# Projecting attention features in native float32 on TensorE's two halves, in place of a block-diagonal split product

## The chip, the cores and the metric

The kernel runs as one program on one core of a Trainium2 chip. Its time is the device time of one execution in microseconds (us), as the median of three executions. The core's engines are TensorE (PE for its matmuls and PEld for its weight loads in the profile), VectorE (DVE), ScalarE (ACT), GpSimd (POOL) and the SyncE queue (SP), which issues all DMAs of the kernel before the change.

## The reference

The inputs are q, k, v of shape (4 batches, 8 heads, 576 positions, 64), omega (128 features x 64), and the weights of two feed-forward layers (512 to 2048 to 512). What is computed is linear attention with random features, followed by the two layers on all 2304 tokens:

```python
def phi(x):                      # x is q or k, scaled by 64 ** -0.25
    proj = einsum('bhsd,md->bhsm', x, omega)
    h = proj - sum(x * x) / 2
    return exp(h - max(h)) / sqrt(m)
kv  = einsum('bhsm,bhsd->bhmd', phi(k), v);  z = sum(phi(k), axis=2)
num = einsum('bhsm,bhmd->bhsd', phi(q), kv)
den = einsum('bhsm,bhm->bhs', phi(q), z) + 1e-06
x = num / den                    # then transposed to (2304, 512)
h = x @ w_in;   x = (h * clip(h + 3, 0, 6) / 6) @ w_out      # layer 1
h = x @ w2_in;  x = (h * sigmoid(1.702 * h)) @ w2_out        # layer 2
```

## The kernel before

**Tiles.** The 576 positions of a batch are cut into 512 main ones (four blocks of 128) and 64 leftover ones. Main positions of each batch are one column block of 512 for the layers; the leftovers of all four batches together are a fifth block of 256 columns, which is worked on along with the last batch. The hidden width 2048 is cut into 16 chunks of 128.

**Precision.** Matmuls of the layers run in the fp32r type on split operands: a number is kept as a high part (rounded to fp32r) and a low part (the rest), and a product is three matmuls, high x high, high x low and low x high. The feature projection is done in the same way. The positions of a q or k block arrive as [128 rows, 128 positions], where rows 0 to 63 hold the 64 dimensions of one block of positions and rows 64 to 127 those of another. `bd_hi` and `bd_lo` hold omega as a block-diagonal pair [128, 2, 128], so that one matmul over all 128 rows gives 256 columns: the features of both position blocks, one after the other. Half of that operand is zeros. `T` (lines 266 and 267) makes the high and low parts of a head's q and k on VectorE, `PJ(h, 0)` projects k and `PJ(h, 1)` projects q with six 256-column matmuls each (`project`, line 225), and `features` takes the maximum on VectorE (L231) and four exponentials on ScalarE (L233). `TL` and `PL` are the same for the leftovers. Transposes (`QT` L315, `QTL` L260, `XT` L367, `XTL` L374), the products with v (`KV`, L292 and L300) and the numerators (`NU`, L329 and L338) are native float32 matmuls already. Outputs of 64 partitions are put into the lower and the upper half in turn in `KV` and `NU`; those of L338 all go to the lower half.

**Stages.** The attention of batch 0 runs first, with little else to fill in. Then come the units of the layers: layer 1 for batches 0, 1 and 2, then batch 3 and the leftovers, then layer 2 in the same order, 16 chunks for each. `emit_h` does the first product of a chunk (L439, twelve matmuls of 512 columns), `emit_o` the second product two chunks later (L501). While layer 1 works on batch n, the attention steps of batch n+1 are put between: `side()` is called twice in `emit_h` and twice in `emit_o`, and each call takes one step off the list until it is empty (57 steps). A call lies after six or twelve matmuls of 512 columns, so most steps stand alone between layer matmuls. Weights of both layers are converted during layer 1 (`convert_w`), with work on ScalarE, VectorE and GpSimd; what is not held on chip goes to DRAM and is fetched again.

**Order.** Each engine runs its instructions in one fixed order. The framework settles it when the program is built, from the order of the program and a planned timeline; `tc.issue_after` (`behind` in the code) adds a wish that one instruction is put behind another. PSUM has eight banks of [128, 512]: four in the pool `acc`, four in `psp`. During layer 1 the `acc` banks hold the second product's sums, and `emit_h` and all attention steps share the four banks of `psp`.

**The end.** `put` copies a result out of PSUM into `ob` and stores it. The leftover results (two tiles, each of two batches with 64 positions) are stored by one DMA each into a [2, 64, 512] piece of the output (L534); all other stores write 128 whole rows (L529).

Of the kernel before, what the change touches and what calls it, by code (L numbers as in the profile page):

```python
# [45 lines left out]
def performer_moe_kernel(  # L47
# [13 lines left out]
    nc = tc.nc  # L61
# [17 lines left out]
    TAIL = 12  # L79
    WARM = 8  # L80
    FIRST = 4
    HELD = 10
# [16 lines left out]
    bd_hi = const.tile([P, 2, M], F32R, name="bd_hi")  # L99
    bd_lo = const.tile([P, 2, M], F32R, name="bd_lo")  # L100
# [137 lines left out]
    class Att:  # L238
        def __init__(self, b, x, xl):
            self.b, self.x, self.xl = b, x, xl  # L240
            self.t, self.e, self.kv, self.xt, self.feat = {}, {}, {}, {}, {}

        def TL(self):
            a, self.vl = lqkv.pop(self.b)
            self.lhi = at.tile([P, NPAIR, P], F32R, tag="thi", bufs=2, name="lhi")
            self.llo = at.tile([P, NPAIR, P], F32R, tag="tlo", bufs=2, name="llo")
            self.split_in(self.lhi, self.llo, a)
            self.el = at.tile([P, NPAIR, 2, M], F32, tag="el", name="el")

        def PL(self, g):  # L250
            ps = bank([P, 4, M], "ps")
            for i in range(2):
                j = 2 * g + i
                project(ps[:, 2 * i:2 * i + 2, :], self.lhi[:, j, :], self.llo[:, j, :])
            features(ps, self.el[:, 2 * g:2 * g + 2].rearrange("p i j m -> p (i j) m"))

        def QTL(self):
            ps = bank([P, NPAIR, P], "ps")
            for i in range(NPAIR):
                nc.tensor.transpose(ps[:, i, :], self.el[:, i, 0, :], ident)  # L260
# [4 lines left out]
        def split_in(self, hi, lo, a):  # L265
            nc.vector.tensor_copy(hi, a)
            nc.vector.tensor_tensor(out=lo, in0=a, in1=hi.bitcast(F32), op=ALU.subtract)

        def T(self, h):
            a = qkv[self.b, h // 2][0][:, h % 2]  # L270
            hi = at.tile([P, 2, 2, P], F32R, tag="thi", bufs=2, name="thi")
            lo = at.tile([P, 2, 2, P], F32R, tag="tlo", bufs=2, name="tlo")
            self.split_in(hi, lo, a)
            self.t[h] = (hi, lo)

        def PJ(self, h, j):
            hi, lo = self.t[h]
            ps = bank([P, R, M], "ps")
            for g in range(2):
                project(ps[:, 2 * g:2 * g + 2, :], hi[:, j, g, :], lo[:, j, g, :])  # L280
            e = at.tile([P, R, M], F32, tag=f"e{j}", bufs=2, name="e")
            self.feat[h] = features(ps, e)
            self.e[h, j] = e

        def KV(self, h):
            i, p0 = h // 2, 64 * (h % 2)
            vv = qkv[self.b, i][1]
            e = self.e.pop((h, 0))
            ps = bank([P, D + 1], "ps")
            for r in range(R):  # L290
                for m0 in (0, 64):
                    nc.tensor.matmul(  # L292
                        out=ps[m0:m0 + 64, :],
                        lhsT=e[:, r, m0:m0 + 64],
                        rhs=vv[:, h % 2, r, :],
                        start=(r == 0),
                        stop=False,
                    )
            for m0 in (0, 64):
                nc.tensor.matmul(  # L300
                    out=ps[m0:m0 + 64, :],
                    lhsT=self.el[p0:p0 + SL, i, 1, m0:m0 + 64],
                    rhs=self.vl[p0:p0 + SL, i, :],
                    start=False,
                    stop=True,
                )
            kv = at.tile([P, D + 1], F32, tag="kv", bufs=4, name="kv")
            nc.scalar.copy(kv, ps)
            self.kv[h] = kv

        def QT(self, h):
            e = self.e.pop((h, 1))
            ps = bank([P, R, P], "ps")
            for r in range(R):
                nc.tensor.transpose(ps[:, r, :], e[:, r, :], ident)  # L315
            t = at.tile([P, R, P], F32, tag="qpt", bufs=1, name="qpt")
            nc.scalar.copy(t, ps)
            self.e[h, "t"] = t

        def NU(self, h):  # L320
            i = h // 2
            t = self.e.pop((h, "t"))
# [57 lines left out]
    def att_steps(a):  # L380
        b = a.b
        st = [lambda: a.T(0)]
        for h in range(H + 2):
            if h < H:
                st.append(lambda h=h: a.PJ(h, 0))
                st.append(lambda h=h: a.PJ(h, 1))
                if h + 1 < H:
                    st.append(lambda h=h: a.T(h + 1))
            if h == 0:
                st.append(lambda: a.TL())  # L390
            if h <= 1:
                st.append(lambda h=h: a.PL(h))
# [121 lines left out]
    def put(l, i, d, ps, per):  # L514
# [53 lines left out]
    for e in range(2):  # L568
        o0 = 64 * e
        rows = slice(o0, o0 + 64)  # L570
        oth = slice(64 - o0, 128 - o0)
        nc.vector.tensor_copy(bd_hi[rows, e, :], omt[rows, :])
        nc.vector.tensor_tensor(
            out=bd_lo[rows, e, :],
            in0=omt[rows, :],
            in1=bd_hi[rows, e, :].bitcast(F32),
            op=ALU.subtract,
        )
        nc.vector.tensor_copy(bd_hi[oth, e, :], zero_r[oth, :].bitcast(F32))
        nc.vector.tensor_copy(bd_lo[oth, e, :], zero_r[oth, :].bitcast(F32))  # L580

# [40 lines left out]
    lp = None  # L622

    def side():
        if todo:
            todo.pop()()

    for u in range(len(units) + LAG):
        while fetches and fetches[0][0] <= u + AHEAD:
            fetch_w(*fetches.pop(0)[1:])  # L630
        if u < len(units):
            l, n, c = units[u]
            if l == 0 and c == 0 and n + 1 < B:
                xblk[0, n + 1] = new_x(n + 1)
                steps = att_steps(Att(n + 1, xblk[0, n + 1], xl))
                todo = steps[::-1]
            if (l, n, c) == (0, B - 2, NC - 1):
                while todo:
                    side()
# [19 lines left out]
            if c == NC - 1:  # L659
                while todo:  # L660
                    side()
# [60 lines left out]
```

## Time and profile before

| | us |
|---|---|
| median of three executions | 982.69 (982.96, 978.67, 982.69) |
| the profiled execution | 980.37 |
| its span, first to last instruction | 978.6 |
| busy: PE / PEld / DVE / ACT / POOL | 946.1 / 783.8 / 477.7 / 415.5 / 152.4 |

"Busy" counts the time in which an engine has an instruction in it. A matmul's recorded time includes its way through the array, so two matmuls that follow closely overlap in the records, and the spacing of their starts tells the throughput. A native float32 matmul leaves two records of LDWEIGHTS and two of MATMUL, a float32 transpose and an fp32r matmul leave one: 32 heads with eight matmuls at L292 give 512 records. The profiled execution is 1.8 us longer than its span, and the median of the three is 2.3 us above the profiled execution.

### The profile page before, as it was taken

What the parts mean: (1) busy time and instruction counts of PE and PEld (TensorE: products, weight loads), DVE (VectorE), ACT (ScalarE), POOL (GpSimd) and SP (SyncE); (2) the same over time, 40 slices, a digit from 0 to 9 for tenths busy, and PEclk for the clock granted to TensorE, in tenths of its full rate; (3) what the DMA queues carried; (4) which work ended last, traced back from release to release, by engine and by line L of the source; (5) the groups of instructions that cost most, each with busy time, mean ns of one, the idle gap of its engine ahead of it and who ended that gap; (6) DMA issues with size and microseconds to landing.
All of it is one profiled execution on the core that took longest, in us unless ns stands there. A gap on an engine that the chain in (4) does not pass through costs nothing.

```text
span 978.6 us, 14409 instructions
## 1 busy us (share of the span) xinstructions
PE 946.1 (97%) x5626; PEld 783.8 (80%) x5626; DVE 477.7 (49%) x845; ACT 415.5 (42%) x868; POOL 152.4 (16%) x127
## 2 busy tenths in 40 slices
PE   8799999999999999999999999999999999999994
PEld 6678777788877778778888888888888888888883
DVE  7988988886776875333222222223223222322221
ACT  5976776675655665342222322222123212221221
POOL 0212322334443343030000101020002000000000
PEclk9999999999999999999999999999999999999997
DMA  6666677977788865246333384446335443422301
GB/s 196 249 226 224 214 258 247 370 266 270 270 306 281 288 227 204 86 151 211 120 124 128 129 264 140 134 148 212 131 130 175 130 144 114 150 67 86 108 1 64
DMA packets 54775, 177.23 MB, mean 181 GB/s; under 512 B 5812, under 2 KB 7476, under 8 KB 54708
## 3 DMA queue, kind: packets, MB, share of 16 engines
q1 hardware_dynamic: 54708, 176.32, 52.9%
q8 instruction: 44, 0.72, 0.3%
q14 instruction: 23, 0.19, 0.1%
HBM read 138.55 MB, written 37.75 MB: 180 GB/s over the span
## 4 chain that ended last, share of the span: by engine, by line
PE 74%; DVE 7%; DMA 7%; POOL 5%; ACT 3%; issue 3%; SPq 0%; POOLq 0%; ACTq 0%
PE ps L439 34%; PE o L501 34%; DMA ws1i<-wsn 4%; POOL wsn L211 3%; DVE w L205 3%; PE ps L225 2%; DMA ws1o<-wsn 2%; POOL w L202 2%; DVE mx L231 1%; PE ps L329 1%; ACT w L187 1%; PE ps L292 1%; DVE wtop L193 1%; ACT e L233 0%; DMA qk<-in_qk_dram 0%
## 5 line engine op out<-in xcount | busy, mean ns | idle before, releaser
L439 PE MATMUL ps<-x,wss 128*128 128x512 f32 x1152 | 287.3, 394 | 3.4 <-ACT wss L210 1.9
L439 PEld LDWEIGHTS ps<-x,wss 128*128 128x128 f32 x1152 | 212.2, 188 | 48.0 <-ACT wss L210 3.5
L457 DVE TENSOR_TENSOR ga<-ga,ps 128x512 f32<-128x512 f32 x80 | 50.8, 635 | 252.4 <-ACT ga L456 252.4
L456 ACT ACTIVATE ga<-ps 128x512 f32<-128x512 f32 x80 | 44.4, 554 | 252.3 <-PE ps L439 252.3
L501 PE MATMUL o<-gs,wss 128*128 128x512 f32 (+1 forms) x600 | 137.3, 375 | 1.3 <-ACT gs L459 1.0
L460 DVE TENSOR_TENSOR gs<-ga,gs 128x512 fp32r<-128x512 f32 (+1 forms) x160 | 109.1, 697 | 51.1 <-ACT gs L459 48.1
L501 PE MATMUL o<-wss,gs 128*128 128x512 f32 x540 | 129.8, 390 | 0.0
L501 PEld LDWEIGHTS o<-gs,wss 128*128 128x128 f32 x600 | 102.2, 189 | 20.1 <-ACT gs L459 1.3
L501 PEld LDWEIGHTS o<-wss,gs 128*128 128x128 f32 x540 | 100.7, 188 | 20.5
L459 ACT CAST gs<-ga 128x512 fp32r<-128x512 f32 (+1 forms) x160 | 91.7, 579 | 43.6 <-DVE ga L457 32.4
L202 POOL TENSOR_TENSOR w<-w,wpow 128x512 f32<-128x512 f32 x64 | 77.7, 1234 | 168.0 <-DVE wpow L197 129.1
L452 DVE SCALAR_TENSOR_TENSOR ga<-ga,ps 128x512 f32<-128x512 f32 x80 | 50.1, 629 | 109.3 <-ACT ga L451 109.1
L439 PE MATMUL ps<-x,wsh 128*128 128x512 f32 x384 | 94.7, 393 | 0.5 <-ACT wsh L210 0.5
L451 ACT ACTIVATE ga<-ps,three 128x512 f32<-128x512 f32 x80 | 51.6, 648 | 101.7 <-PE ps L439 101.5
L439 PEld LDWEIGHTS ps<-x,wsh 128*128 128x128 f32 x384 | 70.9, 188 | 15.8 <-ACT wsh L210 0.7
L501 PE MATMUL o<-gs,wsh 128*128 128x512 f32 (+1 forms) x360 | 82.9, 374 | 0.6 <-ACT gs L459 0.4
L205 DVE TENSOR_TENSOR w<-w,wtop 128x512 f32<-128x512 f32 x64 | 75.3, 1188 | 16.3 <-POOL w L202 16.3
L501 PE MATMUL o<-wsh,gs 128*128 128x512 f32 x324 | 78.5, 390 | 0.0
L233 ACT ACTIVATE e<-ps,mx 128x128 f32<-128x128 f32 x220 | 63.4, 386 | 24.6 <-DVE mx L231 24.4
L501 PEld LDWEIGHTS o<-gs,wsh 128*128 128x128 f32 x360 | 61.6, 189 | 12.2 <-ACT gs L459 1.0
L501 PEld LDWEIGHTS o<-wsh,gs 128*128 128x128 f32 x324 | 60.4, 188 | 12.3
L541 POOL TENSOR_TENSOR x<-xr,x 128x512 fp32r<-128x512 f32 x16 | 22.2, 1417 | 264.2 <-ACT x L540 264.2
(123 smaller groups left out, 963.3 us busy)
## 6 DMA issues: line engine op xcount, KB each, us to landing
wss<-ws1i SPq DMA_DIRECT2D x48, 512.0 KB, 3.2
wss<-ws1o SPq DMA_DIRECT2D x40, 512.0 KB, 3.3
wss<-ws0i SPq DMA_DIRECT2D x36, 512.0 KB, 4.9
wraw<-in_w_in_dram SPq DMA_DIRECT2D x32, 512.0 KB, 4.5
wraw<-in_w_out_dram SPq DMA_DIRECT2D x32, 512.0 KB, 5.6
wss<-ws0o SPq DMA_DIRECT2D x30, 512.0 KB, 4.2
ws1i<-wsn SPq DMA_DIRECT2D x16, 512.0 KB, 3.5
ws1o<-wsn SPq DMA_DIRECT2D x16, 512.0 KB, 3.0
```

The costliest lines, as they stand in the source:

```text
L202: nc.gpsimd.tensor_tensor(out=w[:, cols], in0=w[:, cols], in1=q[:, cols], op=ALU.mult)
L205: nc.vector.tensor_tensor(out=wj, in0=wj, in1=a[:, j * DM:(j + 1) * DM], op=ALU.add)
L211: (nc.vector if l == 0 else nc.gpsimd).tensor_tensor(out=s[:, 1], in0=wj, in1=s[:, 0].bitcast(F32), op=ALU.subtract)
L233: act = nc.scalar.activation(out=e[:, r, :], in_=ps[:, r, :], func=AF.Exp, bias=mx[:, r:r + 1])
L439: nc.tensor.matmul(out=ps, lhsT=w[:, wi, kk, :], rhs=x[:, xi, kk, :], start=(m == 0), stop=(m == 3 * NK - 1),)
L451: nc.scalar.activation(out=g, in_=ps, func=AF.Relu, bias=three)
L452: nc.vector.scalar_tensor_tensor(out=g, in0=g, scalar=6.0, in1=ps, op0=ALU.min, op1=ALU.mult)
L456: nc.scalar.activation(out=g, in_=ps, func=AF.Sigmoid, scale=1.702)
L457: nc.vector.tensor_tensor(out=g, in0=g, in1=ps, op=ALU.mult)
L459: nc.scalar.copy(s[:, 0, :], g)
L460: nc.vector.tensor_tensor(out=s[:, 1, :], in0=g, in1=s[:, 0, :].bitcast(F32), op=ALU.subtract)
L501: last = nc.tensor.matmul(out=ps[:, e, :], lhsT=lhsT, rhs=rhs, start=(c == 0 and m == 0 and per == 1), stop=(c == NC - 1 and m == 2 and e ...
```

## The change

Omega is used as it is, in float32, twice one above the other in `omt`; the block-diagonal copies and the splitting of q and k go. A head's q and k are projected in one step. Each product has 64 contracted rows, 128 stationary columns (positions) and 128 moving columns (features); the products of rows 0 to 63 and of rows 64 to 127 go into two PSUM banks and are queued in turn, each put behind the one before. The steps of a batch become 39, spread evenly over the calls of `side()`; the order of `KV` and `QT` is swapped; one more weight tile is held on chip (`HELD` 11); the first weight conversion is put in 10 steps before the end of the first attention instead of 12. The leftover results are stored by one DMA for each batch, on the SP and the ACT queue.

```diff
-    TAIL = 12
+    EB = 3
+    TAIL = 10
-    HELD = 10
+    HELD = 11
-    bd_hi = const.tile([P, 2, M], F32R, name="bd_hi")
-    bd_lo = const.tile([P, 2, M], F32R, name="bd_lo")
-    def project(ps, lhs_hi, lhs_lo):
-        o = ps.rearrange("p a m -> p (a m)")
-        for n, (a, w) in enumerate(((lhs_hi, bd_hi), (lhs_hi, bd_lo), (lhs_lo, bd_hi))):
-            nc.tensor.matmul(
-                out=o, lhsT=a, rhs=w.rearrange("p a m -> p (a m)"), start=(n == 0), stop=(n == 2)
-            )
+    HALVES = (slice(0, D), slice(D, 2 * D))
+
+    def project(ps, n, rows, lhsT):
+        return nc.tensor.matmul(out=ps[:, n, :], lhsT=lhsT, rhs=omt[rows, :], start=True, stop=True)
...
-        def T(self, h):
...
-        def PJ(self, h, j):
-            hi, lo = self.t[h]
-            ps = bank([P, R, M], "ps")
-            for g in range(2):
-                project(ps[:, 2 * g:2 * g + 2, :], hi[:, j, g, :], lo[:, j, g, :])
-            e = at.tile([P, R, M], F32, tag=f"e{j}", bufs=2, name="e")
-            self.feat[h] = features(ps, e)
-            self.e[h, j] = e
+        def PJ(self, h):
+            a = qkv[self.b, h // 2][0][:, h % 2]
+            ps = [bank([P, R, M], "ps") for _ in HALVES]
+            mm = None
+            for j in range(2):
+                for g in range(2):
+                    for p, rows in zip(ps, HALVES):
+                        with behind(mm):
+                            mm = project(p, 2 * j + g, rows, a[rows, j, g, :])
+            e = at.tile([P, 2, 2, 2, M], F32, tag="e", bufs=EB, name="e")
+            for half, p in enumerate(ps):
+                self.feat[h] = features(p, e[:, half].rearrange("p j g m -> p (j g) m"))
+            self.e[h] = e
...
             if 1 <= h <= H:
+                st.append(lambda h=h: a.KV(h - 1))
                 st.append(lambda h=h: a.QT(h - 1))
-                st.append(lambda h=h: a.KV(h - 1))
...
-            nc.sync.dma_start(
-                out=out.rearrange("(b s) e -> b s e", s=S)[2 * d:2 * d + 2, SM:S, :],
-                in_=ob,
-            )
+            for e, eng in enumerate((nc.sync, nc.scalar)):
+                r0 = (2 * d + e) * S + SM
+                eng.dma_start(out=out[r0:r0 + SL, :], in_=ob[e * SL:(e + 1) * SL, :])
...
     def side():
-        if todo:
+        pace[1] += 1
+        while todo and (pace[0] - len(todo)) * 4 * NC < pace[0] * pace[1]:
             todo.pop()()
```

`PL` of the leftovers is changed as `PJ` is (eight products, two banks). Where a block of 16 chunks ends, what is left of the list is emitted at once, as before.

## Rows read from the trace of the kernel before

**Rows 1.** Busy time by stage: stretch, length, busy us (x instructions) by engine, PEclk, DMA share, GB/s.

```profile
0.00:63.00 63.00, 52.72 (x531) 43.29 (x532) 51.35 (x120) 44.90 (x124) 10.00 (x15) 0.97 0.69 233
63.00:440.00 377.00, 369.00 (x2524) 295.83 (x2523) 282.60 (x491) 234.97 (x494) 122.91 (x97) 1.00 0.69 242
440.00:965.20 525.20, 524.37 (x2575) 444.63 (x2573) 143.75 (x235) 135.61 (x251) 19.50 (x16) 1.00 0.41 135
965.20:977.30 12.10, 0.00 (x0) 0.00 (x0) 0.00 (x0) 0.00 (x0) 0.00 (x0) 0.65 0.13 44
```

**Rows 2.** Chain that ended last: start us, us, what; a run in layer 1, and its end.

```profile
581.97 2.72 PE ps L439 x12
...
964.41 0.69 DVE ob L520
```

**Rows 3.** Timeline of PE in layer 1: start us, us, engine, line, operation, tiles, shapes, count.

```profile
388.10 1.53 PE L439 MATMUL ps<-x,wss 128*128 128x512 f32 x6
389.47 0.28 PE L225 MATMUL ps<-bd_hi,thi 128*128 128x256 f32 x1
...
390.18 1.55 PE L439 MATMUL ps<-x,wss 128*128 128x512 f32 x6
...
409.91 3.01 PE L501 MATMUL o<-gs,wsh 128*128 128x512 f32 x12
412.85 0.69 PE L329 MATMUL ps<-kv,qpt 128*64 128x65 f32 x16
413.47 1.66 PE L439 MATMUL ps<-x,wss 128*128 128x512 f32 x6
...
421.22 0.40 PE L338 MATMUL ps<-kv,qtl 128*64 128x65 f32 x4
...
424.41 0.60 PE L367 MATMUL ps<-ident,xt 128*128 128x128 f32 x4
...
426.66 0.73 PE L439 MATMUL ps<-x,wss 128*128 128x512 f32 x2
427.32 0.27 PE L374 MATMUL ps<-ident,xln 64*128 64x64 f32 x1
427.52 1.20 PE L439 MATMUL ps<-x,wss 128*128 128x512 f32 x4
```

**Rows 4.** Groups by line and shape on PE: count, busy us, mean ns of one, idle before.

```profile
L329 PE MATMUL ps<-kv,qpt 128*64 128x65 f32 x416 | 18.5, 229 | 1.1 <-ACT kv L308 1.1
L367 PE MATMUL ps<-ident,xt 128*128 128x128 f32 x52 | 8.3, 282 | 0.3 <-DVE den L351 0.3
L338 PE MATMUL ps<-kv,qtl 128*64 128x65 f32 x52 | 5.2, 222 | 0.0
```

**Rows 5.** Groups on DVE, 63 to 440 us: the splitting of q and k.

```profile
L267 DVE TENSOR_TENSOR tlo<-qk,thi 128x512 fp32r<-128x512 f32 x22 | 16.7, 758 | 0.0
L266 DVE CAST thi<-qk 128x512 fp32r<-128x512 f32 x22 | 11.1, 503 | 3.1 <-PE ps L225 3.1
```

**Rows 6.** Timeline of the first ten us, with the idle time before and what ended it.

```profile
1.44 3.78 PE L560 MATMUL acc<-zero_r 128*128 128x512 f32 x8 [1.44 <-DVE zero_r L556]
3.57 0.43 DVE L266 CAST thi<-qk 128x512 fp32r<-128x512 f32 x1 [1.43 <-DMA qk<-in_qk_dram]
3.92 0.22 DVE L567 TENSOR_SCALAR omt<-omt 128x128 f32<-128x128 f32 x1
...
7.17 0.43 DVE L266 CAST thi<-qk 128x512 fp32r<-128x512 f32 x1 [1.41 <-DMA qk<-in_qk_dram]
...
8.96 1.14 ACT L233 ACTIVATE e<-ps,mx 128x128 f32<-128x128 f32 x4 [6.94 <-DVE mx L231]
```

**Rows 7.** Busy time, columns as in Rows 1: a stretch in the first attention.

```profile
47.20:50.60 3.40, 3.40 (x27) 2.77 (x25) 2.96 (x9) 2.89 (x4) 0.00 (x0) 0.50 0.70 267
```

**Rows 8.** Source line of the leftover stores (first and last start us at the end), issue durations in ns.

```profile
L534 SPq DMA_DIRECT2D out_dram<-ob x2: 527/597/667, 964.4 to 965.1; - x2
```

**Rows 9.** Source line of the 128-row stores L529: from issue to landing.

```profile
DMA to landing us min/median/max: 2.1/3.6/5.7
```

More of the change, by code (lines that the diff above doesn't have):

```diff
@@ L240, in __init__, with PL @@
             self.b, self.x, self.xl = b, x, xl
-            self.t, self.e, self.kv, self.xt, self.feat = {}, {}, {}, {}, {}
-        def TL(self):
+            self.e, self.kv, self.xt, self.feat = {}, {}, {}, {}
+        def PL(self):
             a, self.vl = lqkv.pop(self.b)
[L245 to L255, printed above, removed]
+            self.el = at.tile([P, 2, NPAIR, M], F32, tag="el", name="el")
+            ps = [bank([P, NPAIR, M], "ps") for _ in HALVES]
+            mm = None
+            for i in range(NPAIR):
+                for p, rows in zip(ps, HALVES):
+                    with behind(mm):
+                        mm = project(p, i, rows, a[rows, i, :])
+            for j, p in enumerate(ps):
+                features(p, self.el[:, j])
         def QTL(self):
@@ L259, in QTL @@
             for i in range(NPAIR):
-                nc.tensor.transpose(ps[:, i, :], self.el[:, i, 0, :], ident)
+                nc.tensor.transpose(ps[:, i, :], self.el[:, 0, i, :], ident)
             self.qtl = at.tile([P, NPAIR, P], F32, tag="qtl", name="qtl")
@@ L263, in QTL @@
             self.xln = at.tile([SL, NPAIR, 2, D], F32, tag="xln", name="xln")
-        def split_in(self, hi, lo, a):
-            nc.vector.tensor_copy(hi, a)
-            nc.vector.tensor_tensor(out=lo, in0=a, in1=hi.bitcast(F32), op=ALU.subtract)
-        def T(self, h):
+        def PJ(self, h):
             a = qkv[self.b, h // 2][0][:, h % 2]
[L271 to L274, printed above, removed]
-        def PJ(self, h, j):
-            hi, lo = self.t[h]
-            ps = bank([P, R, M], "ps")
-            for g in range(2):
-                project(ps[:, 2 * g:2 * g + 2, :], hi[:, j, g, :], lo[:, j, g, :])
-            e = at.tile([P, R, M], F32, tag=f"e{j}", bufs=2, name="e")
-            self.feat[h] = features(ps, e)
-            self.e[h, j] = e
+            ps = [bank([P, R, M], "ps") for _ in HALVES]
+            mm = None
+            for j in range(2):
+                for g in range(2):
+                    for p, rows in zip(ps, HALVES):
+                        with behind(mm):
+                            mm = project(p, 2 * j + g, rows, a[rows, j, g, :])
[3 more added lines that the diff above has]
+            self.e[h] = e
         def KV(self, h):
@@ L287, in KV @@
             vv = qkv[self.b, i][1]
-            e = self.e.pop((h, 0))
+            e = self.e[h]
             ps = bank([P, D + 1], "ps")
@@ L293, in KV @@
                         out=ps[m0:m0 + 64, :],
-                        lhsT=e[:, r, m0:m0 + 64],
+                        lhsT=e[:, r % 2, 0, r // 2, m0:m0 + 64],
                         rhs=vv[:, h % 2, r, :],
@@ L301, in KV @@
                     out=ps[m0:m0 + 64, :],
-                    lhsT=self.el[p0:p0 + SL, i, 1, m0:m0 + 64],
+                    lhsT=self.el[p0:p0 + SL, 1, i, m0:m0 + 64],
                     rhs=self.vl[p0:p0 + SL, i, :],
@@ L311, in QT @@
         def QT(self, h):
-            e = self.e.pop((h, 1))
+            e = self.e[h]
             ps = bank([P, R, P], "ps")
             for r in range(R):
-                nc.tensor.transpose(ps[:, r, :], e[:, r, :], ident)
+                nc.tensor.transpose(ps[:, r, :], e[:, r % 2, 1, r // 2, :], ident)
             t = at.tile([P, R, P], F32, tag="qpt", bufs=1, name="qpt")
             nc.scalar.copy(t, ps)
-            self.e[h, "t"] = t
+            self.e[h] = t
         def NU(self, h):
             i = h // 2
-            t = self.e.pop((h, "t"))
+            t = self.e.pop(h)
             kv = self.kv[h]
@@ L381, in att_steps @@
         b = a.b
-        st = [lambda: a.T(0)]
+        st = []
         for h in range(H + 2):
             if h < H:
[L385 to L388, printed above, removed]
+                st.append(lambda h=h: a.PJ(h))
             if h == 0:
-                st.append(lambda: a.TL())
-            if h <= 1:
-                st.append(lambda h=h: a.PL(h))
+                st.append(lambda: a.PL())
             if h == 2:
@@ L567, in performer_moe_kernel @@
     nc.vector.tensor_scalar(out=omt, in0=omt, scalar1=scale, scalar2=None, op0=ALU.mult)
[L568 to L580, printed above, removed]
     xl = xp_.tile([P, NK, B * SL], F32, name="xl")
@@ L622, in performer_moe_kernel @@
     lp = None
+    pace = [0, 0]
     def side():
-        if todo:
+        pace[1] += 1
+        while todo and (pace[0] - len(todo)) * 4 * NC < pace[0] * pace[1]:
             todo.pop()()
@@ L636, in performer_moe_kernel @@
                 todo = steps[::-1]
+                pace[:] = len(todo), 0
             if (l, n, c) == (0, B - 2, NC - 1):
                 while todo:
-                    side()
+                    todo.pop()()
                 actx.close()
@@ L660, in performer_moe_kernel @@
                 while todo:
-                    side()
+                    todo.pop()()
         if u >= LAG:
```

## The prediction

> **What bounds the kernel now.** I read the busy time by stage first. There the reader is to see four stretches. From 440 to 965 us, layer 2 and the end of layer 1, PE is busy 524.4 of 525.2 us. From 63 to 440 us, layer 1 with the attention of the next batch between, it is busy 369.0 of 377. In the first 63 us it is busy 52.7, with VectorE at 51.4 and ScalarE at 44.9. And from 965.2 to 977.3 us no engine works at all, while DMAs move 44 GB/s at a share of 0.13 [rows 1]. The chain of waits says the same: layer matmuls one behind the other (twelve of 512 columns in 2.72 us, so 0.2267 us each), up to one copy on VectorE at 964.4 us [rows 2]. So the time is what TensorE is given to do, plus a start in which it waits, plus 12 us of storing at the end. A change can gain in these three places only.
>
> **The end.** Of the two leftover stores the second is issued at 965.1 us [rows 8], and its bytes flow until 977.3 us. A share of 0.13 of 16 DMA engines is two engines [rows 1]; the destination of that transfer is [2, 64, 512], so I read it as one engine for each batch. The stores of 128 whole rows, twice the bytes of a new one, land 2.1 us after issue at best, 3.6 us in the median [rows 9]. A new store is 64 whole rows, from 64 partitions, so I expect it to be spread as they are. The queues are empty by then: I take 2.5 us, so the last bytes land at 967.6 in place of 977.3 us: -9.7 us. Ends: -8.6 (3.6 us) to -10.1 (2.1 us); 0 if the spreading fails. ScalarE issues one store after its own last copy (SP takes 0.53 to 0.67 us for an issue [rows 8]); both are issued at once, and this hides in the same wait.
>
> The Trainium skill has a rule against this part: DMA: Bandwidth & Descriptors, Rules for kernel authors, says that transfers to two disjoint partition halves serialize on the same 16 engines and should be one transfer of 128 partitions. By that rule alone the part would give nothing; the row above with a share of 0.13 speaks against it here, since this one transfer does not use the 16 engines.
>
> **The projection on TensorE.** Before: from the six layer matmuls at 388.10 to those at 390.18 us lie 2.08 us, of which 6 x 0.2267 = 1.36 are theirs; so `PJ(h, j)` takes 0.72 us, and a head 1.44 us for q and k [rows 3].
>
> After: eight products, 16 records, of 128 columns and 64 rows. No row shows this form, so I bound it.
> Length of a record: at L338, where nothing overlaps, four records of 65 columns take 0.40 us with 0.222 for one, so (0.40 - 0.222) / 3 = 0.059 us each; the transposes, 128 columns and one record each, are spaced (0.60 - 0.282) / 3 = 0.106 us [rows 3, 4]. Scaling 0.059 by 128/65 gives 0.117. I take 0.11.
> Overlap: at L329, with outputs in the two halves in turn, 16 records take 0.69 us with 0.229 for one, 0.031 us each, half of the 0.059 where the halves don't alternate [rows 3, 4]. So halves of the output columns run two at a time. Halves of the contracted rows, with results in two banks, are no row's case; I take the nearest row, two at a time: 8 x 0.11 = 0.88 us. The other end is none: 16 x 0.11 = 1.76 us.
> Switching: a step that uses part of the array costs more than its records. One L374 record of 64 rows between layer matmuls: from 426.66 to 427.52 us are 0.86 us, less two layer matmuls 0.41, of which some 0.06 is its own; so 0.35 us for going in and out. The L329 step: from 409.91 to 413.47 us are 3.56, less 12 x 0.2267 = 0.84, less 16 x 0.03 = 0.36 us [rows 3]. The old projection used the whole array and paid none of this; the new one pays 0.36 us in each step.
> Sum: 0.88 + 0.36 = 1.24 us for a head, 0.20 less than before. Between layer matmuls lie 3 batches x (8 heads + 1 for the leftovers, whose matmuls change alike) = 27 such steps: -5.4 us. Where the planned order puts a layer matmul into the middle of a step, another 0.36 us is paid; I allow for two or three: -4.5 us. Ends: 27 x (1.76 + 0.36 - 1.44) = +18 and 27 x (0.85 + 0.35 - 1.44) = -6.5 us.
>
> What the Trainium skill states on this lies between: TensorE: Matmul & The Clock Gate, Part 3: Packing small matmuls, has row tiles run concurrently, with four of them measured at 3.07 times one, 77% of full overlap. An estimate from that figure of the page is 0.88 / 0.77 + 0.36 = 1.50 us for a head, +1.7 us in all.
>
> **VectorE relieved.** The splits cost 16.7 + 11.1 us between 63 and 440 us for q and k alone [rows 5], a tenth of VectorE's 282.6 busy us there [rows 1]. TensorE's idle time in this stretch is 377 - 369 = 8 us, so at most that can come back. TensorE waits there partly for weight and activation work that stands in the same VectorE queue. I take -2 us, between -6 and 0. Against it stands a new demand: a step now takes two of the four banks of `psp` at once, and eight exponentials (4 in 1.14 us [rows 6]) stand on ScalarE in a row, with the first product's activation behind them. The layer's second product comes two chunks later and hides such a delay; if it is not hidden, it costs up to half of that run each time (a rival below).
>
> **The first attention.** Its first exponential runs at 8.96 us. VectorE comes to its maximum late, because the split of the next qk half waits 1.41 us for a DMA at the head of its queue. Omega is there at 3.92 us and scaled at 4.15; the eight warm-up matmuls end their run at about 5.2 us [rows 6]. Now nothing stands between omega's scaling and `PJ(0)`: with starts from about 4.9 us and, at the slow clock of the start, twice 0.88 us, the first bank is ready at 6.6 us, the maximum (about 0.7 us) at 7.3: some 1.7 us earlier. After that VectorE (51.4 of 63 us busy) loses nine times 0.43 + 0.72 us of splitting in this batch, 10 us, but ScalarE with 44.9 us has nothing taken from it and becomes the limit; I take 3 us of the ten. A granted clock of 0.50 between 47.2 and 50.6 us, that is 1.2 GHz, followed a stretch in which TensorE waited [rows 7]; if that wait goes, half of 3.4 us comes back, and I count 1.3. Together -6 us, between 0 and -10.
>
> **At nothing.** `HELD` 11 takes away some fetches; TensorE waits for none in the long stretch (524.4 of 525.2 us busy at a DMA share of 0.41 [rows 1]). If the cover went, it could only gain. The swap of `KV` and `QT`, `TAIL`, and even spacing move the same instructions; spacing puts the last numerators and transposes of a batch closer to the end of a block, where the next block needs them: 0 in the sum, +2 us a block (three blocks), about the length of one such chain, as an end; -3 as the other.
>
> **Sum.** -9.7 - 4.5 - 2 - 6 = -22.2 us, against the profiled execution's own 980.4 us (span 978.6): 958.2 us. The median of the runs shown lies 2.3 us above that execution; I put half of it on: 959 us.
>
> **Rivals.**
> 1. The row halves don't overlap. For it: no row shows row halves at once. Against it: column halves do. Projection +18, end -9.7; in the first attention nine heads more at 0.68 us eat the 6 us gained; VectorE's relief 0, since TensorE is the later one: +8.3 in place of -22.2, so 959 + 30.5 = 989 us, slower. Between the two ends the sum crosses zero where a good quarter of the full overlap (8.3 / 30.5) is reached; below that it is slower. Chance 0.06.
> 2. They overlap in part, as the 1.50 us estimate would have it: +1.7 in place of -4.5: 959 + 6.2 = 965 us. 0.12.
> 3. Banks and the run of eight exponentials: each of 27 steps stalls TensorE by 0.5 us, less than one half's four exponentials: +13 us: 972 us. For it: `psp` is shared by all. Against it: `emit_o` needs no bank of it. 0.13.
> 4. The end does not shorten, because a 64-row store is no better spread: 969 us. Against it: the 128-row stores. 0.04.
> 5. Larger gains in the start and of the 8 us idle: -10 and -6: 951 us. 0.13.
> Forecast: 0.52, with its own range of 954 to 964.
>
> **Numbers.** A measurement of this kernel tells 0.5%, about 5 us, from no change. The forecast, rivals 2, 4 and 5 are faster, and so is 3; rival 1 is slower. With room for what I have not thought of: faster 0.89, within 0.5% 0.05, slower 0.06. The range 949 to 971 leaves out rival 1, most of what lies beyond rival 3, and the far end of rival 5.
>
> **What would show it.** The end: the last stretch without engine work is about 3 us long in place of 12, at a higher DMA share. The projection: 16 records in one step, pairs of starts a few ns apart, some 0.11 us to the next pair; about 1.24 us between layer matmuls. The start: first exponential at about 7.3 us, no stretch at half clock near 47 us. VectorE: under 260 us in the stretch of layer 1 with attention. I am wrong if the records of the two halves start 0.11 us apart each, if PE's idle time grows between 60 and 440 us, or if the last store still takes over 5 us.

## The result, and the profile after

The changed kernel takes 989.74 us (median of four, 988.28 to 990.32), against 982.22 us for the kernel before beside it: a ratio of 1.0073 with a 95% interval of 1.0052 to 1.0094. It is slower by 0.7%; the forecast was 959 us.

Busy time by stage in the changed kernel, with the columns of [rows 1]:

```profile
0.00:63.00 63.00, 51.45 (x577) 41.98 (x577) 41.80 (x93) 47.95 (x129) 9.82 (x15) 0.84 0.70 242
63.00:440.00 377.00, 360.44 (x2513) 278.58 (x2514) 249.30 (x424) 223.97 (x471) 111.53 (x88) 0.97 0.67 230
440.00:983.20 543.20, 543.20 (x2682) 460.05 (x2680) 150.49 (x248) 144.11 (x270) 28.02 (x24) 1.00 0.39 130
983.20:988.00 4.80, 0.31 (x2) 0.00 (x0) 0.69 (x1) 0.26 (x1) 0.00 (x0) 0.97 0.63 203
```

The end did what was forecast: the last stretch is 4.8 us, with the last copies in it and a DMA share of 0.63. The loss lies ahead of it. Between 63 and 440 us VectorE has 33 us less to do than in [rows 1], and yet TensorE stands idle for 16.6 us in place of 8: one of the signs by which the prediction was to be known as wrong. Its granted clock is 0.97 there and 0.84 in the first 63 us. With the end 9.7 us shorter and the time 7.5 us longer, the rest has lost some 17 us.

**The stores at the end**, as a source line (columns of [rows 8]): two on each of two queues.

```profile
L522 SPq DMA_DIRECT2D out_dram<-ob x2: 473/510/547, 983.5 to 984.3; - x2
L522 ACTq DMA_DIRECT2D out_dram<-ob x2: 571/626/682, 983.5 to 984.3; - x2
```

**The new products**, from the timeline of the first ten us and then from that of PE in layer 1 (columns of [rows 6] and [rows 3]):

```profile
5.14 0.27 PE L226 MATMUL ps<-omt,qk 64*128 64x128 f32 x1
...
5.15 0.27 PE L226 MATMUL acc<-omt,qk 64*128 64x128 f32 x1
...
5.25 0.27 PE L226 MATMUL ps<-omt,qk 64*128 64x128 f32 x1
...
5.26 0.27 PE L226 MATMUL acc<-omt,qk 64*128 64x128 f32 x1
```

```profile
193.99 1.16 PE L226 MATMUL ps<-omt,qk 64*128 64x128 f32 x14
195.08 0.73 PE L425 MATMUL ps<-x,wss 128*128 128x512 f32 x2
195.74 0.48 PE L226 MATMUL ps<-omt,lqk 64*128 64x128 f32 x2
197.31 1.16 PE L226 MATMUL ps<-omt,lqk 64*128 64x128 f32 x14 [1.08 <-DVE ga L438]
```

The two row halves start some 10 ns apart, the next pair 0.11 us later: the halves overlap fully. But a step is often cut: one product (two records), some layer matmuls, then the other seven (14 records). Eleven of the 27 steps stand so, and a twelfth is cut into four and four (two more are cut by other work of the attention).

**The waits of TensorE** between 63 and 450 us (us in total, times, longest), and three windows around the second of them (columns of [rows 1], answering [rows 7]):

```profile
PE ps L226 <- ACT e L232: 5.4, 3, 4.7
PE ps L358 <- DVE den L342: 3.9, 1, 3.9
PE ps L306 <- DVE ga L438: 2.5, 1, 2.5
PE ps L226 <- DVE ga L438: 1.8, 2, 1.1
```

```profile
184.00:188.20 4.20, 0.48 (x3) 0.05 (x1) 2.98 (x8) 2.20 (x3) 0.56 (x1) 1.00 0.68 201
...
189.00:192.40 3.40, 3.40 (x11) 2.70 (x11) 1.91 (x5) 2.12 (x3) 2.08 (x3) 0.50 0.92 304
199.20:206.00 6.80, 6.34 (x24) 5.25 (x25) 3.07 (x5) 6.59 (x21) 1.28 (x1) 0.50 0.75 271
```

TensorE has 0.48 us of work in 4.2 us; then it is busy, but at a clock of 0.50, that is 1.2 GHz. In the kernel before I count one such stretch between the first and the last microseconds (3.4 us, [rows 7]); here I count seven, 41.0 us together, each around or behind waits of TensorE.

What stood in the way at 184 us is in the chain of waits from 179 to 189 us (start, us, what):

```profile
181.84 3.28 DVE w L206 x2
185.12 0.03 ACTq L187
185.15 0.05 issue
185.19 1.11 ACT wtop L187
186.30 0.02 issue
186.32 0.43 DVE wmag L190
186.75 0.07 DVE den L342
...
188.34 0.08 issue
188.42 0.63 PE ps L358 x4
189.04 0.51 PE ps L365 x3
189.55 0.72 PE ps L425
```

The denominators `den` (0.15 us of VectorE) need the numerators, which TensorE made at 181 us. They run at 186.7, because three instructions of a weight conversion stand before them in VectorE's fixed order: L206 twice, 3.3 us of work here (one takes 0.66 us at best and 1.62 in the median of 64), and L190, which waits 1.2 us for ScalarE's copy L187, which in turn had waited 4.33 us for L206. Behind `den` are the last transposes of the batch (L358) and behind those the next block. The longest wait, at 330 us, is of the same kind on ScalarE: its conversion copy L211 waits for an earlier store of converted weights, and the exponentials that free TensorE's bank stand behind it. Between the two stand copies of layer 1's results (L508), the second of which waits 2.0 us for a store of such results; so this wait is not the conversion's alone.

```profile
325.39 4.08 DMA ws1i<-wsn
...
329.55 0.62 ACT wsn L211
330.17 0.51 ACT ob L508
...
330.69 2.02 DMA xs<-ob
...
332.82 0.60 ACT ob L508
333.42 0.58 ACT ga L437
333.99 1.04 ACT e L232 x4
...
335.08 1.01 PE ps L226 x5
```

### The profile page after: what moved, and what is told of

The parts are those of the page before. It is cut to its first block, busy times and chain, and to the rows that moved or that the text cites. A ratio compares the mean times of both kernels' runs of the same rounds, so it can differ in the third digit from the quotient of the medians.

```text
span 988.0 us, 14612 instructions
## 1 busy us (share of the span) xinstructions
PE 955.4 (97%) x5770; PEld 780.6 (79%) x5770; DVE 442.3 (45%) x765; ACT 416.3 (42%) x868; POOL 149.4 (15%) x127
## 4 chain that ended last, share of the span: by engine, by line
PE 69%; DVE 9%; ACT 8%; DMA 7%; POOL 5%; issue 3%; POOLq 0%; SPq 0%; ACTq 0%; DVEq 0%
PE ps L425 32%; PE o L487 32%; DMA ws1i<-wsn 5%; DVE w L206 3%; POOL wsn L212 3%; PE ps L226 2%; POOL w L203 2%; ACT e L232 2%; ACT wtop L187 2%; ACT w L188 1%; DMA ws1o<-wsn 1%; DVE mx L230 1%; DVE wtop L194 1%; DVE gs L446 1%; PE ps L283 1%
## 5 line engine op out<-in xcount | busy, mean ns | idle before, releaser
L425 PE MATMUL ps<-x,wss 128*128 128x512 f32 x1056 | 267.3, 399 | 1.6 <-DVE ga L438 1.0
L425 PEld LDWEIGHTS ps<-x,wss 128*128 128x128 f32 x1056 | 197.1, 190 | 44.3 <-DVE ga L438 1.2
L487 PE MATMUL o<-gs,wss 128*128 128x512 f32 (+1 forms) x600 | 143.0, 381 | 0.0
L487 PEld LDWEIGHTS o<-gs,wss 128*128 128x128 f32 x600 | 103.7, 191 | 20.4 <-issue 0.4
L425 PE MATMUL ps<-x,wsh 128*128 128x512 f32 x480 | 118.8, 393 | 0.3 <-ACT e L232 0.3
L487 PEld LDWEIGHTS o<-wss,gs 128*128 128x128 f32 x540 | 100.7, 188 | 20.5
L425 PEld LDWEIGHTS ps<-x,wsh 128*128 128x128 f32 x480 | 88.7, 188 | 19.3 <-ACT e L232 0.7
L203 POOL TENSOR_TENSOR w<-w,wpow 128x512 f32<-128x512 f32 x64 | 75.1, 1195 | 149.4 <-DVE wpow L198 101.6
L206 DVE TENSOR_TENSOR w<-w,wtop 128x512 f32<-128x512 f32 x64 | 77.8, 1234 | 26.6 <-POOL w L203 26.6
```

What stands on the lines that cost most here:

```text
L203: nc.gpsimd.tensor_tensor(out=w[:, cols], in0=w[:, cols], in1=q[:, cols], op=ALU.mult)
L206: nc.vector.tensor_tensor(out=wj, in0=wj, in1=a[:, j * DM:(j + 1) * DM], op=ALU.add)
L425: nc.tensor.matmul(out=ps, lhsT=w[:, wi, kk, :], rhs=x[:, xi, kk, :], start=(m == 0), stop=(m == 3 * NK - 1),)
L487: last = nc.tensor.matmul(out=ps[:, e, :], lhsT=lhsT, rhs=rhs, start=(c == 0 and m == 0 and per == 1), stop=(c == NC - 1 and m == 2 and e ...
```

## The experiments

"Tail" below is the two leftover stores alone; "block n" runs from the first layer matmul (L425, before L439) of batch n to that of the next, worked out from PE's timeline. The last column is the time at half clock between the first 4 us and 940 us. All in us. The median is that of all executions, everything behind it is from the one that was profiled; that one lies up to 3.3 us from its median (tail_only 3.2 below, not_in_turn 3.3 above), so a difference of 1 or 2 us in one cell says little.

| kernel | median | first attention | block 0 | 1 | 2 | 3 | layer 2 | half clock |
|---|---|---|---|---|---|---|---|---|
| before | 982.2 | 37.8 | 143.9 | 122.5 | 127.1 | 131.2 | 401.5 | 3.4 |
| after | 989.7 | 39.7 | 149.8 | 132.2 | 131.4 | 128.6 | 401.4 | 41.0 |
| tail_only | 974.5 | 38.9 | 141.6 | 123.2 | 128.2 | 131.3 | 401.4 | 6.8 |
| pace_only | 984.4 | 38.9 | 147.9 | 125.9 | 124.5 | 128.7 | 401.4 | 6.8 |
| native_old_pace | 980.1 | 38.6 | 138.6 | 134.4 | 128.6 | 131.2 | 401.5 | 27.3 |
| old_pace_qt_first | 983.6 | 38.5 | 140.4 | 133.6 | 130.8 | 131.3 | 401.4 | 30.7 |
| not_in_turn | 984.8 | 46.3 | 142.9 | 130.5 | 131.7 | 128.5 | 401.5 | 30.7 |
| banks_swapped | 980.9 | 38.6 | 145.2 | 130.2 | 130.1 | 128.6 | 401.4 | 27.3 |
| no_conv_before | 965.9 | 37.3 | 144.0 | 121.1 | 123.9 | 131.2 | 401.5 | 3.4 |
| no_conv_after | 969.7 | 39.7 | 145.8 | 122.4 | 125.5 | 128.5 | 401.5 | 23.9 |
| late_conv_before | 973.4 | 39.4 | 142.4 | 124.7 | 128.0 | 131.2 | 401.5 | 10.2 |
| late_conv_after | 990.2 | 38.7 | 150.0 | 132.2 | 131.5 | 128.5 | 401.5 | 30.7 |
| late_conv_old_pace | 979.5 | 38.7 | 137.9 | 131.3 | 129.9 | 131.2 | 401.5 | 17.1 |
| held_conv_before | 977.2 | 39.2 | 142.3 | 121.1 | 123.9 | 136.6 | 409.3 | 13.7 |
| held_conv_after | 980.8 | 38.9 | 146.1 | 122.4 | 125.4 | 132.4 | 409.3 | 20.5 |
| held_conv_swapped | 978.5 | 37.9 | 145.8 | 122.4 | 125.5 | 133.3 | 406.9 | 20.5 |
| held_conv_old_pace | 966.0 | 38.1 | 137.9 | 122.3 | 122.3 | 136.7 | 401.5 | 13.7 |

**The stores alone** (tail_only): the kernel before with the loop over two stores of 64 rows.

> The kernel before with the two leftover stores of the change and nothing else. Theory of the end (a [2, 64, 512] destination keeps a store on two DMA engines): the last stretch without engine work shrinks from 12 to 3 us, the time falls by 9.5 us to 972 to 973. Rival (64-row stores are no better spread): within 1 us of before.

974.49 us, ratio 0.9912 (0.9893 to 0.9931), 1.5 us above the text of the theory and far from the rival's. Its last stretch is the one of the changed kernel:

```profile
964.80:969.50 4.70, 0.21 (x1) 0.00 (x0) 0.69 (x1) 0.17 (x1) 0.00 (x0) 0.75 0.62 199
```

So the stores give some 8 us (7.8 by the medians, 8.6 by the ratio), and all else together costs 989.7 - 974.5 = 15.2.

**The spacing alone** (pace_only): the kernel before with

```diff
-        if todo:
+        pace[1] += 1
+        while todo and (pace[0] - len(todo)) * 4 * NC < pace[0] * pace[1]:
             todo.pop()()
...
```

> The kernel before with the even spacing of the 57 attention steps and nothing else. Theory A (even spacing costs: the last numerators and transposes of a batch come where the next block already waits for them): slower by 8 to 20 us, with TensorE's waits on the transposes L367 at about 180, 300 and 430 us. Rival B (the two banks that a projection step takes at once are the cause, not the spacing): within 2 us of before. Rival C (spreading evens VectorE's load): faster by 3 to 6 us.

984.38 us, ratio 1.0026 (1.0014 to 1.0039): some 2 us slower, next to rival B's text. By itself it is not the cause.

**The change without the spacing** (native_old_pace): the same lines put back in the changed kernel.

> The changed kernel with side() taking one step a call again, as before. Theory A (spacing is the cause of the loss): 968 to 974 us, that is the forecast's gain less what the first attention did not give. Rival B (the two banks are the cause): 984 to 990 us, with TensorE still waiting in L226 for ScalarE's exponentials at the start of each block.

980.13 us, ratio 0.9979 (0.9965 to 0.9993), between the two texts. The spacing costs 9.6 us with the new projection, and 2 with the old one; the new projection costs 5.6 (over tail_only) without the spacing. The parts do not add, so no part has a price of its own.

**Halves one after the other** (not_in_turn): the loops turned, all products of one half first.

```diff
-            for j in range(2):
-                for g in range(2):
-                    for p, rows in zip(ps, HALVES):
+            for p, rows in zip(ps, HALVES):
+                for j in range(2):
+                    for g in range(2):
...
```

> The changed kernel with the eight products of one half queued first and those of the other half behind them. If the halves run two at a time only when they alternate: a step is 1.76 + 0.36 in place of 0.88 + 0.36 us, 27 steps between layer matmuls 24 us more, so 1010 to 1016 us. If they did not overlap in the changed kernel either: within 2 us of it, 988 to 992. If the wait for the second bank is what a step costs, the four products that come first hide it and the loss is smaller: 995 to 1005.

984.75 us, ratio 1.0018 (0.9996 to 1.0039): a miss for all three texts. One step in the timeline:

```profile
142.92 1.71 PE L226 MATMUL ps<-omt,qk 64*128 64x128 f32 x16
```

The step is half a microsecond longer than the whole one of the changed kernel: its 16 records lie some 0.1 us apart each, so halves that are not queued in turn do not overlap. The first attention is 6.6 us longer, and still the kernel is 5 us faster (in the median; the profiled execution is 1.7 us faster). So the length of a projection is not what decides, and an explanation from TensorE's own time falls.

**The banks exchanged** (banks_swapped): the first product into the bank asked for last.

```diff
-                    for p, rows in zip(ps, HALVES):
+                    for p, rows in zip(ps[::-1], HALVES):
...
-            for half, p in enumerate(ps):
+            for half, p in enumerate(ps[::-1]):
...
```

> The changed kernel, with the first product of a step put into the bank that the step asks for last, so that it cannot be planned before both banks are there. Theory of the second bank (in the changed kernel 9 of 27 steps between layer matmuls are cut into one product and the other seven, 0.63 us each, and some wait there): the cut steps go, 5 to 8 us faster than the changed kernel, 982 to 985 us. Rival (the steps are cut by the planned order for another reason, or the stall moves to the start of the step): within 2 us of 989.7.

980.86 us, ratio 0.999 (0.9974 to 1.0005), 8.9 us faster than the changed kernel, more than expected. But ten steps were still cut into one product and seven, so not for the reason that I had given. The work is the same; only the planned order of all engines differs.

**KV and QT** (old_pace_qt_first): native_old_pace with `QT` ahead of `KV` as before.

> The changed kernel with one step a call and with QT before KV again, as in the kernel before; against native_old_pace (980.1 us) it differs in that order alone. Theory: the numerators now follow the q transposes with one step less between, and wait 2.6 to 3.1 us at a time for ScalarE's copy of them: 976 to 978 us. Rival (the copy is late because it stands behind a weight conversion on ScalarE, whatever the order): within 1.5 us of 980.1.

983.61 us, ratio 1.0011 (0.9998 to 1.0023), 3.5 us slower than native_old_pace. Both texts missed; the swap is no cause of the loss.

**Without the conversion of layer 2's weights** (no_conv_before: with the new stores; no_conv_after). Both leave that conversion out, and layer 2 runs on layer 1's weights.

```diff
-    conv = [(l, c) for l in range(2) for c in range(NC)]
+    conv = [(0, c) for c in range(NC)]
...
```

> The kernel before with the new stores, without the conversion of layer 2's weights: layer 2 runs on layer 1's. It serves as the base of no_conv_after. 968 to 974 us: TensorE hardly waits for the conversion here (4.5 us of idle time after 181 us).

> The changed kernel without the conversion of layer 2's weights (layer 2 runs on layer 1's). Theory A (the added waits of TensorE are waits for ScalarE and VectorE work that stands behind weight conversions in their queues): blocks 1 and 2 of layer 1, 132 and 131 us long in the changed kernel, come down to within 3 us of no_conv_before's, and the gap between the two kernels falls from 15 us (989.7 to 974.5) to 6 or less, what is left being the first 190 us. Rival B (banks, pacing and the steps' own cost): the gap stays at 11 to 16 us.

965.88 us, 2 below the text's range, and 969.73 us. Without it the changed kernel gains 20.0 us, the old one 8.6, and the gap of 15.2 us shrinks to 3.9, as theory A had it. In blocks 1 and 2 TensorE is busy nearly all the time; here the changed kernel first, then no_conv_after (columns of [rows 1]):

```profile
189.50:321.70 132.20, 127.71 (x878) 98.98 (x877) 86.67 (x139) 79.84 (x167) 51.86 (x41) 0.96 0.78 269
321.70:453.10 131.40, 126.60 (x890) 98.56 (x890) 56.71 (x105) 58.91 (x145) 17.76 (x15) 0.97 0.45 150
...
185.50:307.90 122.40, 121.14 (x878) 94.26 (x877) 44.05 (x91) 49.21 (x128) 0.00 (x0) 1.00 0.37 121
307.90:433.40 125.50, 124.27 (x891) 96.67 (x891) 43.95 (x91) 49.67 (x131) 0.28 (x1) 1.00 0.34 110
```

With the same matmuls, these two blocks are 15.7 us longer in the changed kernel: TensorE stands idle 6.8 us more, and is busy 8.9 us more, of which half of the 16.5 us at half clock that lie there makes 8.3. So most of the loss needs the conversion beside the attention. But DMA traffic goes too, and work is missing; the next runs do all of the work.

**The conversion later in the program** (late_conv_after, late_conv_before, late_conv_old_pace):

```diff
-            elif l == 0:
-                convert_next(NC + -(-(u - NC + 1) // (B - 1)))
+            elif (l, n) == (0, B - 1):
+                convert_next(NC + c + 2)
```

> The changed kernel with one edit: layer 2's weights are converted in the last block of layer 1, one chunk of weights for each chunk of work, in place of one for every three chunks of the last three blocks. All work is done. Theory A (in blocks 1 and 2 the attention's copies and the activations wait on ScalarE, VectorE and GpSimd behind weight conversions, TensorE behind them, and then at half clock): blocks 1 and 2 become as long as without the conversion, 122 and 126 us in place of 132 and 131, the last block at most 5 us longer: 970 to 977 us. Rival B (what matters is where the planned order happens to fall, and any change of it moves the kernel by several us, in either direction): blocks 1 and 2 stay within 3 us of their 132 and 131, 984 to 992 us. Rival C (the conversion is moved to where it hurts as much): blocks 1 and 2 shorter by 8 us or more, the last one longer by the same, 984 to 990 us.

> The kernel before with the two new leftover stores, and the same edit: layer 2's weights converted in the last block of layer 1. Theory A: this kernel lost about 8.6 us to the conversion (974.5 with, 965.9 without); 966 to 970 us, and the kernel with the new projection stays 3 to 8 us behind it, since the loss in the first 190 us is not touched. Rival B (planned order): 972 to 980 us. Rival C: within 2 us of 974.5, the last block longer by what blocks 1 and 2 gain.

> The changed kernel with the steps of the attention taken one at each call as before, and layer 2's weights converted in the last block of layer 1. With the conversion in blocks 1 to 3 it took 980.1 us, its blocks 1 and 2 134.4 and 128.6 us. Theory A: both become 122 to 126 us; 967 to 974 us. Rival B (planned order): 976 to 985 us. If the pacing matters only beside conversions, it comes within 2 us of the same kernel with even spacing.

990.18, 973.39 and 979.46 us: no gain. It reads like rival B, but the conversion had not moved. (In the program the first of its 16 chunks stands in the last chunk of block 0 and stays there, since `convert_next(c + 2)` reaches one beyond layer 1's; the edit moves the other 15.) Here is its copy L211 (L210 in the old program; durations in ns, then first and last start), in late_conv_after, in the changed kernel and in tail_only:

```profile
L211 ACT CAST wsn<-w x32: 611/620/685, 165.5 to 361.5; 128x512 fp32r<-128x512 f32 x32
```

```profile
L211 ACT CAST wsn<-w x32: 617/621/686, 166.7 to 362.2; 128x512 fp32r<-128x512 f32 x32
```

```profile
L210 ACT CAST wsn<-w x32: 606/620/654, 180.4 to 384.8; 128x512 fp32r<-128x512 f32 x32
```

The framework orders an engine by its planned timeline and pulls work forward from later in the program. The rows show more: in tail_only the first of these copies starts when block 0 is over (180.4 of 180.5), in the changed kernel at 166.7, 23 us before block 0 ends. In all kernels with the new projection and a conversion that is not held back I find it between 165 and 169 us, in all with the old one between 179 and 182.

**The conversion held back** (held_conv_after, held_conv_before, held_conv_swapped, held_conv_old_pace): as above, with each conversion's first instructions on ScalarE and VectorE put behind the activation of the chunk before.

```diff
-                convert_next(c + 2)
+                convert_next(min(c + 2, NC))
...
+                convert_next(NC + c + 2, *gelu)
...
-            emit_h(l, n, c, side)
+            gelu = emit_h(l, n, c, side)
...
```

> The changed kernel; layer 2's weights are converted in the last block of layer 1, and each conversion's first instruction on ScalarE and VectorE is put behind the activation of the chunk before it, so that the planned order cannot pull it forward. All work is done. Theory A (the loss is waits behind the conversions in blocks 1 and 2): blocks 1 and 2 as without the conversion, 122 and 126 us in place of 132 and 131; block 0 to the second block's start 185 to 189 us; the last block at most 5 us longer: 970 to 977 us. Rival B (where the planned order falls): blocks 1 and 2 together shorter by less than 6 us, 982 to 992 us. Rival C (it hurts as much in its new place): the last block is longer by what is saved before, 984 to 992 us.

> The kernel before with the two new leftover stores, and the conversion held back in the same way. Theory A: 966 to 971 us (965.9 without any conversion of layer 2, 974.5 with it spread), and held_conv_after stays 3 to 8 us behind. Rival B: 972 to 980 us. Rival C: 973 to 978 us, the last block longer.

> held_conv_after with the first of the two products put into the bank that was asked for last. With the conversions spread this edit gained 8.8 us. Theory A: with no conversion beside blocks 1 and 2 the waits that it moved are not there, so it gains at most 3 us over held_conv_after: 968 to 977 us. Rival D (the order of the banks itself decides how long a projection holds up TensorE): it gains 6 us or more again, all of it in blocks 0 to 2.

> held_conv_after with the attention's steps taken one at each call as before. With the conversions spread this gained 9.6 us. Theory A: blocks 1 and 2 122 to 126 us with either spacing, and the total within 4 us of held_conv_after: 967 to 977 us. Rival B: 976 to 985 us, and 6 us or more ahead of held_conv_after.

held_conv_after: 980.78 us, ratio 0.9968 (0.9953 to 0.9984). Now the copies run from 440.4 to 656.5 us, and blocks 1 and 2 are 122.4 and 125.4 us, what theory A had said and 15.8 us less than in the changed kernel. The total misses A's 970 to 977, since the conversion comes too late for layer 2: it is 7.9 us longer, and the timeline of PE shows for what it waits there.

```profile
649.11 4.37 PE L425 MATMUL ps<-x,wsh 128*128 128x512 f32 x12 [3.73 <-DMA wsh<-ws1i]
...
660.23 2.11 PE L425 MATMUL ps<-x,wss 128*128 128x512 f32 x8 [2.20 <-DMA wss<-ws1i]
```

held_conv_before: 977.23 us, ratio 0.9926 (0.99 to 0.9952): the same 7.9 us in layer 2, 5.3 in block 3, and 6.4 gained in blocks 1 and 2; so slower than tail_only, within the texts of rivals B and C and 6 us above theory A's. held_conv_after stays 3.6 us behind it, in place of 15.2.

held_conv_swapped: 978.51 us, ratio 0.996 (0.994 to 0.998). Exchanging the banks now gives 2.3 us, less than the executions of either kernel spread, and blocks 1 and 2 do not change by more than 0.1 us. So its 8.9 us needed the conversion beside the attention, as theory A says, though the total lies 1.5 us above A's range; rival D falls.

held_conv_old_pace: 965.95 us, ratio 0.9823 (0.9797 to 0.9848), the best of all, ahead of both kernels: 23.8 us faster than the changed kernel, 8.5 faster than tail_only. Theory A had 967 to 977, and at most 4 us between the two spacings (rival B 6 or more, but at 976 to 985); they lie 14.8 apart: 7.8 in layer 2, which waits for no weights here (the last copy L211 runs at 635.0 us, not 656.5), and 7.1 in layer 1 as a whole. Three of its blocks by stage (0 from 63 us on, 1 and 2):

```profile
63.00:176.00 113.00, 110.88 (x797) 86.60 (x796) 91.94 (x167) 77.42 (x152) 28.71 (x24) 1.00 0.68 233
176.00:298.30 122.30, 122.30 (x890) 96.92 (x888) 45.06 (x93) 50.03 (x128) 0.00 (x0) 1.00 0.39 128
298.30:420.60 122.30, 122.30 (x890) 96.95 (x889) 45.30 (x94) 52.54 (x133) 2.82 (x4) 1.00 0.37 122
```

TensorE never stands in blocks 1 and 2. So even spacing costs something with layer 2's conversion gone, too. In block 0 layer 1's own conversion runs beside the attention and could act in the same way; that was not tried. Against held_conv_before, which has the old projection and the same spacing, this kernel is 11.3 us faster, 7.8 of them in layer 2 and 4.4 in block 0. So the new projection by itself is no loss.

## Why the prediction was wrong

**The end: right.** Forecast -9.7 us; from the last matmul's start to the end of the span are 4.9 us in place of 14.6 in the profiles, and by the medians of tail_only the gain is 7.8. The Trainium skill's rule against it (DMA: Bandwidth & Descriptors, Rules for kernel authors) speaks of two transfers that share the same 16 engines, and does not reach this case: two stores on disjoint halves beat one, whose share had been 0.13.

**The overlap of the halves: right, its sum not.** The spacing of 0.11 us for a pair is that of the forecast, and a whole step costs 1.30 us for 1.24. So rivals 1 and 2 fall. (The 3.07 times one that the Trainium skill states for four row tiles, in TensorE: Matmul & The Clock Gate, Part 3: Packing small matmuls, is 77% of full overlap; two row tiles overlap fully here.) But I allowed two or three cut steps at 0.36 us; twelve are cut, and one costs 0.62 + 1.31 = 1.93 us, or 2 x 0.86 = 1.72 for the one cut in the middle. By these, an estimate is 15 x 1.30 + 11 x 1.93 + 1.72 = 42.5 us against 27 x 1.44 = 38.9: +3.6 in place of -4.5. Where TensorE never waits, blocks 1 and 2 take 244.6 us with the new projection (held_conv_old_pace) and 245.0 with the old (held_conv_before): on TensorE's time the new one is worth nothing there.

**VectorE relieved: the step that failed.** It said that at most the 8 us of idle time could come back, between -6 and 0. That bound took the order of the rest as fixed. VectorE did lose 33 us of work, but layer 2's conversion started 14 us earlier, beside the end of block 0's attention; short links of the attention came to stand behind conversion instructions that take 1.6 us each or wait for ScalarE or a store. TensorE's idle time between 63 and 440 us doubled, from 8.0 to 16.6 us. Blocks 0 to 2 cost 20.4 us more than in tail_only, block 3 2.7 less. In block 0, from 63 us on, the room on VectorE was filled again: it is busy 109.3 us with the conversion of layer 2 and 94.8 without it (after, no_conv_after), 106.0 and 103.8 with the old projection (tail_only, no_conv_before). That the loss needs the conversion beside the attention is shown: without it, and with it held back, the gap of 15.2 us is 3.9 and 3.6 (no_conv and held_conv, the second with all work done). That the relief is what let the planned order pull it forward is only read from the start times and these sums: `HELD`, `EB` and `TAIL`, which change with the projection, were never run by themselves.

**At nothing: failed with it.** I priced the spacing at 0, with +2 a block as an end, by the length of one chain at the block's end. Alone it costs 2 us in all; with the new projection 9.6. The bound was the chain's own work. The chain at 184 us has 0.15 us of `den` in it and took 4 us longer, for what stands ahead on VectorE. The swap of `KV` and `QT` at nothing was harmless.

**The first attention: the start right, the sum not.** The first exponential was forecast at 7.3 us and runs at 6.85, 8.96 before:

```profile
6.85 1.14 ACT L232 ACTIVATE e<-ps,mx 128x128 f32<-128x128 f32 x4 [4.83 <-DVE mx L230]
```

Yet the first layer matmul comes at 39.7 us, 37.8 before. Over all runs it comes between 37.3 and 39.4 us with the old projection (six kernels) and between 37.9 and 39.7 with the new one queued in turn (ten): of the 6 us forecast nothing is seen. VectorE is 10 us less busy in the first 63 us, TensorE no earlier: it waits 3.1 us for ScalarE's copy `qpt` and 3.7 us for `den`, and behind these it runs at half clock. I had expected the half clock of [rows 7] to go; there is more of it: 3.4 to 6.8 us of the first 63 with the old projection, 13 us or more in every kernel with the new one.

**The rivals.** Rival 3 was nearest in kind: banks held by exponentials are in the longest wait (L226 behind ACT `e`). But I spread it as 0.5 us over 27 steps, for the exponentials' own length; it came as a few waits of 2 to 5 us, for conversions in front of them. None had the sum above 982 for this reason. Rival 1, on the slower side, had 989 us, the time that was measured; but it was bound to halves that do not overlap, and they do, so it met the number by luck.

**What stays open.** How much of the loss is the waits and how much the half clock behind them is known for blocks 1 and 2 alone (6.8 and 8.9 us, above), not for the first attention and block 0. With the conversion held back 3.6 us remain between the two kernels, and they go with the even spacing, since with the old spacing the new projection is 11.3 us ahead. Of the 14.8 us that the spacing costs there, 7.8 lie in layer 2; why the other 7 arise was not found.

## What to carry to other kernels

Where a planned order fills the engines, work taken off one engine leaves a hole that other work can be pulled into: before pricing relief, look at what stands next in that engine's queue, how long it takes and what it waits for. A short link of the critical chain costs what stands in front of it, not its own length, so price a moved step by the longest instruction, with its wait, that can come to stand before it. Background work is put where it does not hurt by an explicit order on the engines, and the trace must show that it moved; its place in the program alone did nothing here.

## What the hardware showed that I had not expected

Products of 64 rows in the two row halves, native float32, 128 columns each, overlap fully when they are queued in turn: a pair each 0.11 us. Queued one half after the other they do not: 16 records take 1.71 us in place of 1.16. Going into the half array and out of it makes them no better here: it costs some 0.4 us each time (1.30 - 8 x 0.11), so that one product alone costs 0.62 us between layer matmuls. And TensorE's granted clock was 0.50 in seven stretches of 3.4 to 10.2 us, 41.0 us together, around and behind waits of 1 to 5 us, in the middle of a kernel in which it is 97% busy.
